# Attention over a small memory and a channel mix: nine tokens a partition, 32x64 tiles, one PSUM pool

## The chip, the core and the metric

The kernel runs on one core of a Trainium2 chip. A core has TensorE (PE, matmuls; its weight loads are listed as PEld), VectorE (DVE), ScalarE (ACT), GpSimd (POOL) and SyncE (SP). They run at the same time, each works through its own instructions in order, and they wait for each other by semaphores. 16 DMA engines move data between DRAM and the on-chip memory SBUF. TensorE writes its results to PSUM, from where DVE or ACT fetch them. The metric is the device time of one execution in microseconds.

## What is computed

Inputs are q, k, v of 8 batches x 8 heads x 576 tokens x 64, and phi of 8 x 8 x 576 x 32, all float32. Per batch and head, the attention goes over 32 memory slots:

```python
a = exp(phi - max(phi)); a = a / (sum_over_tokens(a) + 1e-09)
k_m = einsum('bhsm,bhsd->bhmd', a, k)
v_m = einsum('bhsm,bhsd->bhmd', a, v)
scores = q @ k_m.T / sqrt(64)
attn = softmax(scores)            # over the 32 slots
x = attn @ v_m                    # then heads side by side: (8, 576, 512)
```

Then a channel mix works on x, with x_prev the token before (zeros for the first):

```python
xk = mu_k * x + (1 - mu_k) * x_prev
xr = mu_r * x + (1 - mu_r) * x_prev
k = maximum(xk @ w_k, 0)          # w_k 512 x 1024
v = k * k @ w_v                   # w_v 1024 x 512
out = sigmoid(xr @ w_r) * v       # w_r 512 x 512
```

Each token needs its predecessor within its batch, and nothing else ties tokens of the channel mix together.

## The kernel before

**Two halves that are woven into each other.** `attention(b)` gives the small steps of one batch, `channel_mix(c)` sixteen groups of matmuls for one of nine chunks of 512 tokens: eight of keys (`pk`, L528), four of gates (`pr`, L542), four of values (`pv`, L561). A chunk is not a batch: chunk 1 needs batches 0 and 1. The transposed inputs of the channel mix, `xkT` and `xrT`, are a ring of four batches.

**The order is written out by hand.** Tables `STEADY` and `FIRST` give each step of a batch a position, counted in groups of the channel mix; all are sorted by it and issued. Since every engine keeps that order, a step that waits holds up all that stands behind it on its engine. After each name, letters say which PSUM pool its tiles come from: three tiles "at", two "pk" (shared with the keys), three "pv" (shared with gates and values). `busyN` steps are matmuls on zeros (L217), whose result nobody reads.

**Loads.** Of k and v, 512 tokens lie four to a partition on 128 partitions, and a tail of 64 tokens on 64 partitions as a fifth slot (L132 and L136). q lies six tokens to a partition on 96 partitions (L143), phi as k. Those of batch 0's phi go through SP's queue (L122, L125), all others through POOL's, which also turns q, k, v and the weights from float32 into bfloat16. At the start the order is k, q, v of batch 0, w_k in two parts, w_r, then phi, k, q of batch 1, w_v, v of batch 1. Tiles of q, k, v and phi exist twice, so batch b + 2 is loaded (step `load`) when batch b is done with them.

**One batch.** `exp` makes `em` = exp(phi) on ACT (L257, and L258 for the tail). `kv` (or `k` and `v` apart) multiplies it with k and v, on 128 rows x 32 columns of the array, a head's 32 slots each (L273). `z` sums `em` over tokens with a matmul against ones (L283), a reciprocal gives `rz`. `nk` scales the keys by it (L292), `tk` transposes them (L314, L317). `q0` to `q3` transpose q, two heads each (L334 on TensorE, the copy at L338); for batches 6 and 7 `qx` does it by DMA on SP (L326). `s0`, `s1` make scores of four heads, in two halves of 288 tokens, and their exp (L351, L355). `l0` to `l3` sum over the slots with a matmul and take Ln (L365, L367), `r0z` or `h0z` exponentiate its negative (L372), `w` or `y` multiply (L379): that is the softmax.

For batches 2 to 7, `nv` scales the values and masks them so that two heads' values stand side by side in 128 columns (L303). `x0` to `x3` multiply: two matmuls, each on 64 rows (two heads) x 128 columns (L392), which ACT copies out as `x` (L396). DVE then takes differences of neighbours (`dd`, L405 to L408) and mixes (`k0d` and the like, L417, L418).

For batches 0 and 1, the mix goes into the values instead: `nkx`, `nrx` multiply the values with mu and 1 - mu (L427), `mk0` to `mr3` multiply the weights of attention with both, and add the shifted one in PSUM (L449, L453), and the result is copied to `xkT` and `xrT` (L458).

**Channel mix.** ACT makes relu of the keys (L532), DVE the square (L533). The gate is exp, Ln, exp on ACT (L547 to L550). DVE multiplies gate and value (L563), and SP stores `o` (L509), the last two tiles with ACT's help.

Of the kernel before, what the change touches and what calls it, by code (L numbers as in the profile page):

```python
# [10 lines left out]
F32 = mybir.dt.float32  # L11
BF16 = mybir.dt.bfloat16
# [5 lines left out]
STEADY = [("exp", -20), ("q2", -16), ("q3+a", -15), ("kv+v", -14), ("z+v", -12), ("nk", -12), ("nv", -12),  # L18
          ("q0", -11), ("q1+a", -11), ("tk+v", -11), ("s1+aa", -8), ("s0+va", -8), ("load", -6),
          ("l0+k", -6), ("l1+k", -5), ("l3+a", -5), ("r0z", -5), ("w0", -3), ("l2+a", 1), ("r1z",  # L20
          1), ("w1", 1), ("x3+ak", 4), ("x0+av", 4), ("x2+vv", 6), ("x1+aa", 6), ("dd", 6), ("r0d",
          8), ("k2d", 11), ("k0d", 13), ("r2d", 22)]
FIRST = {
    0: [("exp", -62), ("z+k", -56), ("busy1_653415", -56), ("mub", -55), ("k+k", -53), ("mu", -48), ("nk",
        -46), ("tk+v", -44), ("q0+v", -43), ("q1+a", -40), ("q3+a", -40), ("s0+a", -39), ("q2+k",
        -38), ("l0+a", -35), ("h0z", -35), ("l1+a", -32), ("busy2_658043", -27), ("mum0", -27),
        ("s1+kv", -25), ("h1z", -25), ("v+v", -24), ("l3+v", -24), ("y0", -24), ("y1", -24),
        ("l2+v", -22), ("h2z", -22), ("busy2_100606", -20), ("h3z", -19), ("nkx", -15), ("load+a",
        -8), ("y2", -7), ("y3", -7), ("busy2_335180", -5), ("mk1+a", -5), ("mk0+kk", -5), ("mk2+aa",
        -4), ("mum1", -3), ("busy1_305423", -2), ("mk3+vv", -1), ("nrx", -1), ("mr2+aa", 2),  # L30
        ("busy1_343727", 3), ("mr0+vv", 3), ("mr1+ka", 4), ("mr3+av", 4)],
    1: [("exp", 5), ("z+a", 7), ("k+a", 9), ("q0+v", 9), ("q2+k", 9), ("nk", 9), ("q1+k", 9), ("q3+a", 9),
        ("tk+v", 9), ("s0+ak", 9), ("s1+va", 9), ("l0+v", 10), ("l1+k", 10), ("l3", 10), ("h0z",
        10), ("y0", 12), ("l2+a", 13), ("v+k", 13), ("h1z", 13), ("nrx", 13), ("nkx", 13), ("y1",
        13), ("h2z", 13), ("y2", 13), ("h3z", 13), ("y3", 13), ("mr0+va", 15), ("mk0+kv", 15),
        ("mr1+ka", 15), ("mk1+vv", 15), ("mr3+kk", 15), ("mk2+aa", 15), ("mk3+vv", 15), ("mr2+av",
        15), ("load+k", 16)],
    2: [("exp", -4), ("q0", -1), ("q1+v", -1), ("q3+a", 0), ("z+k", 0), ("kv+v", 0), ("nk", 0), ("tk+v",
        1), ("q2", 1), ("s0+kv", 2), ("s1+va", 2), ("l0+v", 3), ("l1+a", 3), ("load+k", 3), ("r0z",
        4), ("w0", 5), ("nv", 5), ("l3+a", 5), ("l2+v", 5), ("r1z", 6), ("x0+a", 8), ("w1", 9),  # L40
        ("x1+av", 10), ("x2+aa", 10), ("x3+kk", 10), ("dd", 12), ("k0d", 13), ("k2d", 13), ("r0d",
        13), ("r2d", 21)],
    3: [("exp", -4), ("z+a", -2), ("kv+v", -1), ("nk", -1), ("nv", 0), ("q0+v", 1), ("tk+a", 2), ("q1+v",
        3), ("q3", 3), ("q2", 4), ("s0+ka", 4), ("s1+ak", 5), ("l1+a", 5), ("l2+v", 5), ("l0+v", 5),
        ("l3+k", 5), ("r0z", 5), ("w0", 5), ("r1z", 5), ("w1", 6), ("x0+ka", 7), ("x1+va", 7),
        ("x2+vv", 8), ("x3+kk", 8), ("dd", 9), ("k2d", 9), ("load+k", 9), ("k0d", 11), ("r2d", 13),
        ("r0d", 15)],
    6: [("exp", -23), ("qx", -21), ("kv+v", -15), ("z+v", -12), ("nk", -12), ("nv", -12), ("tk+v", -11),
        ("load+k", -11), ("s1+va", -9), ("s0+va", -9), ("l1+k", -6), ("l0+k", -5), ("r0z", -5),
        ("l2+k", -5), ("l3+a", -4), ("w0", -3), ("r1z", 1), ("w1", 1), ("x1+av", 3), ("x0+vv", 5),  # L50
        ("x3+aa", 6), ("x2+vv", 6), ("dd", 7), ("r0d", 7), ("k0d", 12), ("k2d", 13), ("r2d", 19)],
    7: [("exp", -19), ("z+k", -12), ("kv+a", -12), ("nk", -12), ("tk+v", -11), ("nv", -11), ("qx", -8),
        ("s0+va", -8), ("s1+ak", -8), ("load+k", -8), ("l1+k", -6), ("l0+k", -6), ("r0z", -5),
        ("w0", -4), ("l2+a", -4), ("l3+a", -4), ("r1z", -4), ("w1", -4), ("x0+va", -1), ("x3+aa",
        -1), ("x2+vv", 5), ("x1+av", 5), ("dd", 7), ("r0d", 9), ("k0d", 12), ("k2d", 13), ("r2d",
        20)],
}
LOADS = {None: ("phi", "k", "v", "q"), 2: ("phi", "k", "q", "v"), 3: ("phi", "k", "q", "v"), 4: ("phi", "k", "q", "v")}
ORDER = ('phi', 'k', 'q', 'wv', 'v')

NQ = 6
JT = (0, 2, 4, 1, 3, 5)
NB = 4
TAIL = 512
# [3 lines left out]
def kernel(  # L71
# [23 lines left out]
    NT = S - TAIL  # L95
    HALF = S // 2
    QR = S // NQ
# [11 lines left out]
    NJ = NB + 1  # L109
    kvs = [const.tile([128, 2, H, NJ, D], BF16, name=f"kv{i}") for i in range(2)]  # L110
    qs = [const.tile([QR, H, NQ, D], BF16, name=f"q{i}") for i in range(2)]
    ems = [const.tile([128, NJ, H, M], BF16, name=f"em{i}") for i in range(2)]
# [6 lines left out]
    def load_phi(b, eng):  # L119
        phm = ld.tile([128, H, NB, M], F32, name="phm", tag="phm")  # L120
        pht = ld.tile([NT, H, M], F32, name="pht", tag="pht")
        eng.dma_start(  # L122
            out=phm.rearrange("p h j m -> p h (j m)"),
            in_=phi[b, :, 0:TAIL, :].rearrange("h (p j) m -> p h (j m)", j=NB))
        eng.dma_start(out=pht, in_=phi[b, :, TAIL:S, :].rearrange("h s m -> s h m"))  # L125
        loads[b] = {"phm": phm, "pht": pht}

    def load_rows(dst, src, parts=1):
        n = H // parts
        for i in range(parts):  # L130
            h = slice(i * n, (i + 1) * n)
            nc.gpsimd.dma_start(  # L132
                out=dst[:, h, 0:NB, :].rearrange("p h j d -> p h (j d)"),
                in_=src[h, 0:TAIL, :].rearrange("h (p j) d -> p h (j d)", j=NB))
            if i == 0:
                nc.gpsimd.dma_start(out=dst[:NT, :, NB, :],  # L136
                                    in_=src[:, TAIL:S, :].rearrange("h s d -> s h d"))

    def load_q(b, parts=1):
        n = H // parts  # L140
        for i in range(parts):
            h = slice(i * n, (i + 1) * n)
            nc.gpsimd.dma_start(  # L143
                out=qs[b % 2][:, h].rearrange("p h j d -> p h (j d)"),
                in_=q[b, h].rearrange("h (p j) d -> p h (j d)", j=NQ))

    def load_batch(b):
        for what in LOADS.get(b, LOADS[None]):
            if what == "phi":
                load_phi(b, nc.gpsimd)  # L150
            elif what == "q":
                load_q(b)
            else:
                load_rows(kvs[b % 2][:, "kv".index(what)], (k, v)["kv".index(what)][b])

    load_phi(0, nc.sync)
    load_rows(kvs[0][:, 0], k[0])
    load_q(0, 2)
    make_identity(nc, identity)
# [453 lines left out]
```

## Time and profile before

Three runs: 223.22, 223.40 and 223.44 us. One execution was profiled.

| | us |
|---|---|
| median of the runs | 223.4 |
| span of the profiled execution, first to last instruction | 219.9 |
| PE busy | 202.9 |
| ACT busy | 161.5 |
| DVE busy | 138.8 |
| first matmul (L283) starts | 6.45 |
| first keys of chunk 0 (L528) that run on end | 23.04 |
| first keys of chunk 1 | 52.55 |
| last product of DVE (L563) starts | 215.99 |

The time of a run has some 3.5 us more than the span, which lie around the first and the last instruction. A profile has a row of instructions for each engine: from it come the busy time of an engine, its idle time with what ended it, and the chain of waits, which goes back from the last instruction to whatever released it. Matmuls overlap, and the profile models their ends; a mean of 379 ns for a 512-column matmul does not say that one follows another at that distance. In the chain, four dense ones take 0.86 us.

The DMA queue of POOL moved 20.91 MB in 35,248 packets, its packets took 64.1% of the span of 16 engines. SP's and ACT's moved the 9.44 MB of output and batch 0's phi. Over the span DRAM was read at 38.54 MB: q, k, v and the weights are twice as large there as in SBUF.

### The profile page before, as it was taken

How to read it: one execution, taken by the hardware profiler on the slowest of the kernel's cores; microseconds unless marked ns; L12 is line 12 of the kernel's file. 1: busy time of each engine (PE TensorE's matmuls, PEld its weight loads, DVE VectorE, ACT ScalarE, POOL GpSimd, SP SyncE). 2: the span in 40 equal slices, each digit the busy share in tenths (PEclk: the TensorE clock that was granted, in tenths of full speed). 3: DMA queues.
4: the chain of work that ended last, by engine and by line, in shares of the span. 5: the costliest groups of instructions: out<-in, count | busy, mean ns of one | idle time of the engine just before them, and what ended most of it. 6: DMA issues, size and time to landing. Idle time of an engine off the chain costs nothing.

```text
span 219.9 us, 4457 instructions
## 1 busy us (share of the span) xinstructions
PE 202.9 (92%) x1698; PEld 99.5 (45%) x1698; DVE 138.8 (63%) x346; ACT 161.5 (73%) x311; POOL 47.7 (22%) x66
## 2 busy tenths in 40 slices
PE   0489997998999998999999999999999999999992
PEld 0244344446444564445444854453444444444442
DVE  3246754189465989787968677868876775425322
ACT  2256678855699849997799789988997866765770
POOL 7643351544440538211600000000000000000000
PEclk9999998799999999999999999999999999999998
DMA  6999999999999999999997700371023033033024
GB/s 139 193 191 207 238 203 203 233 223 285 210 235 196 252 243 206 229 194 289 177 180 165 174 0 3 95 174 32 13 85 97 3 95 95 0 95 98 0 64 127
DMA packets 48021, 32.67 MB, mean 149 GB/s; under 512 B 15624, under 2 KB 42512, under 8 KB 48000
## 3 DMA queue, kind: packets, MB, share of 16 engines
q0 software_dynamic: 35248, 20.91, 64.1%
q1 hardware_dynamic: 12448, 11.15, 19.0%
q10 hardware_dynamic: 304, 0.33, 0.4%
q8 instruction: 13, 0.21, 0.4%
q14 instruction: 8, 0.07, 0.1%
HBM read 38.54 MB, written 9.44 MB: 218 GB/s over the span
## 4 chain that ended last, share of the span: by engine, by line
PE 84%; DMA 5%; DVE 4%; POOL 2%; ACT 2%; issue 1%; POOLq 0%
PE pv L561 28%; PE pk L528 28%; PE pr L542 15%; DMA kv<-in_v_dram 5%; PE kvps L273 3%; PE qtps L334 2%; PE nops L392 2%; PE zps L365 2%; PE scps L351 1%; DVE qT L338 1%; PE zps L283 1%; PE mxps L449 1%; PE idle L217 1%; ACT rl L532 1%; POOL kv L132 1%
## 5 line engine op out<-in xcount | busy, mean ns | idle before, releaser
L528 PE MATMUL pk<-xkT,wk 128*128 128x512 bf16 (+1 forms) x320 | 69.0, 358 | 0.5 <-ACT rl L532 0.2
L561 PE MATMUL pv<-wv,sq 128*128 128x512 bf16 (+1 forms) x296 | 65.9, 373 | 0.0
L532 ACT ACTIVATE rl<-pk 128x512 bf16<-128x512 f32 x72 | 43.0, 601 | 26.2 <-PE pk L528 23.9
L563 DVE TENSOR_TENSOR o<-sg,pv 128x512 f32<-128x512 f32 (+1 forms) x37 | 24.1, 671 | 35.1 <-ACT sg L550 20.2
L533 DVE TENSOR_TENSOR sq<-rl 128x512 bf16<-128x512 bf16 x72 | 30.2, 423 | 24.4 <-ACT rl L532 23.8
L561 PEld LDWEIGHTS <-sq 128*128 128x128 bf16 x296 | 28.7, 98 | 32.8 <-issue 0.7
L528 PEld LDWEIGHTS <-wk 128*128 128x128 bf16 x320 | 29.4, 98 | 28.1 <-issue 2.7
L542 PE MATMUL pr<-wr,xrT 128*128 128x512 bf16 x144 | 36.4, 391 | 0.0
L547 ACT ACTIVATE sg<-pr 128x512 f32<-128x512 f32 x36 | 21.5, 609 | 7.0 <-PE pr L542 6.9
L542 PEld LDWEIGHTS <-xrT 128*128 128x128 bf16 x144 | 13.8, 100 | 16.0 <-issue 1.9
L549 ACT ACTIVATE sg<-sg 128x1024 f32<-128x1024 f32 x18 | 19.0, 1057 | 0.6
L550 ACT ACTIVATE sg<-sg 128x1024 f32<-128x1024 f32 x18 | 19.0, 1057 | 0.6
L417 DVE TENSOR_SCALAR mu_d<-diff,mu 128x576 bf16<-128x576 bf16 x48 | 16.0, 376 | 0.1
L396 ACT CAST x<-nops 128x288 bf16<-128x288 f32 x48 | 15.7, 419 | 0.2 <-PE nops L392 0.2
L379 DVE TENSOR_TENSOR atn<-e,lz 128x576 bf16<-128x576 bf16 (+1 forms) x20 | 12.4, 634 | 2.2 <-ACT lz L372 1.9
L367 ACT ACTIVATE lz<-zps 128x288 f32<-128x288 f32 x32 | 11.5, 410 | 0.9 <-PE zps L365 0.9
L338 DVE COPY qT<-qtps 128x576 bf16<-128x576 bf16 x22 | 9.3, 449 | 4.3 <-PE qtps L334 4.3
L355 ACT ACTIVATE e<-scps 128x288 bf16<-128x288 f32 x32 | 10.9, 438 | 1.1 <-PE scps L351 1.1
L372 ACT ACTIVATE lz<-lz 128x576 f32<-128x576 f32 (+1 forms) x20 | 11.4, 592 | 0.2
L257 ACT ACTIVATE em<-phm 128x1024 bf16<-128x1024 f32 x8 | 8.4, 1049 | 3.3 <-DMA phm<-in_phi_dram 3.3
L334 PE MATMUL qtps<-identity,q 96*128 96x96 bf16 x144 | 9.6, 218 | 1.0 <-DMA q<-in_q_dram 1.0
L132 POOL DMA_DIRECT2D kv<-in_v_dram x9 | 7.8, 869 | 9.8 <-issue 4.7
(67 smaller groups left out, 186.1 us busy)
## 6 DMA issues: line engine op xcount, KB each, us to landing
out_dram<-o SPq DMA_DIRECT2D x23, 192.0 KB, 2.5
kv<-in_k_dram POOLq DMA_DIRECT2D x8, 512.0 KB, 12.3
q<-in_q_dram POOLq DMA_DIRECT2D x7, 576.0 KB, 15.0
phm<-in_phi_dram POOLq DMA_DIRECT2D x7, 512.0 KB, 13.5
kv<-in_v_dram POOLq DMA_DIRECT2D x7, 512.0 KB, 14.2
out_dram<-o SPq DMA_DIRECT2D x23, 128.0 KB, 2.5
out_dram<-o SPq DMA_DIRECT2D x23, 64.0 KB, 2.3
wk<-in_moe_w_k_dram POOLq DMA_DIRECT2D x2, 512.0 KB, 12.6
```

The source lines that it names most:

```text
L334: nc.tensor.matmul(ps[:, i, j], rhs=identity[:QR, :QR], is_transpose=True, lhsT=qs[b % 2][:, 2 * pr + i, 2 * j:2 * j + 2, :].rearrange("p ...
L396: nc.scalar.copy(st["x"][:, 2 * c + jj, sl], pss[jj])
L417: nc.vector.tensor_scalar_mul(t[:, i], st["d"][:, pr + i, :], mu1[:, o:o + 1])
L528: nc.tensor.matmul(pk[:, lo:hi], lhsT=wk_sb[:, di, fi * 128:(fi + 1) * 128], rhs=xk_T[:, di, c0:c0 + hi - lo], start=(di == 0), stop=(di = ...
L532: nc.scalar.activation(rl, pk, AF.Relu)
L533: nc.vector.tensor_mul(st["sq"][:, fi, :], rl, rl)
L542: nc.tensor.matmul(pr, lhsT=xr_T[:, di, c0:c0 + 128], rhs=wr_sb[:, di, :], start=(di == 0), stop=(di == ND - 1))
L547: nc.scalar.activation(sg[:, ts % 2], pr, AF.Exp, scale=-1.0)
L549: nc.scalar.activation(sg, sg, AF.Ln, bias=1.0)
L550: nc.scalar.activation(sg, sg, AF.Exp, scale=-1.0)
L561: nc.tensor.matmul(pv[:, cols], lhsT=st["sq"][:, fi, ts * 128:(ts + 1) * 128], rhs=wv_sb[:, fi, cols], start=(fi == 0), stop=(fi == NF - 1))
L563: nc.vector.tensor_mul(o[:, cols], st[ts // 2][:, ts % 2, cols], pv[:, cols])
```

## The change

Every load of q, k, v and phi is laid out anew. A partition has nine consecutive tokens of one head; heads 0 to 3 lie on partitions 0 to 63, heads 4 to 7 on 64 to 127. There is no tail. Each load is done in two halves (phi's second in two pieces), and within heads 4 to 7 phi's are swapped in pairs, so that heads stand where the tiles later want them. Batch 0's phi goes through SP and ACT. The halves of tokens are 320 and 256 now (`HALVES`: five and four of the nine).

Loads at the start come in the order of `PRE`: batch 0's k and q half by half, its v, w_k in three pieces, w_r, phi of batch 1, half of w_v, then k, q, v of batch 1, and the other half of w_v. mu is loaded in one small tile and spread by a matmul with a selection matrix instead of four broadcasting loads.

`kv` takes nine rounds of 64 rows x 32 columns, heads of both halves in turn. q is transposed in 36 pieces of 64 rows x 64 columns instead of 24. `nv` and `nr0`/`nk0` have no mask any more: values stay 64 wide. `x` and `mk`/`mr` multiply head by head, on 32 rows x 64 columns (`head_tiles`).

All PSUM tiles come from one pool of eight, in turn. `qT`, `kmT`, `kbd`, `rz`, `e`, `atn`, `x` have three buffers instead of two, `sq` two instead of one, `o` four instead of three. The order is a list of every step and group (`PLAN`). Chunk 0's values are done in halves of columns, the odd ones early. For batches 0 and 1, most steps exist for each half of the heads. 25 `busy` matmuls instead of nine, 13 of them first of all.

```diff
-STEADY = [("exp", -20), ("q2", -16), ("q3+a", -15), ("kv+v", -14), ("z+v", -12), ("nk", -12), ("nv", -12),
...
+PLAN = [
+    "0:busy1 0:busy1 0:busy1 0:busy1 0:busy1 0:busy1 0:busy1 0:busy1 0:busy1 0:busy1 0:busy1 0:busy1 0:busy1 0:exp0",
+    "6:load 0:hk0 0:z0 0:hn0 0:ht0 0:exp1 0:hq0 0:z1 0:s0 0:hk1 0:busy1 0:l0 0:busy1 0:l1 0:busy1 0:h0z 0:hn1 0:ht1",
+    "0:h1z 0:hq1 0:y0 0:mub 0:mu 0:s1 0:hv0 0:nk0 0:busy1 0:l2 0:nr0 0:busy1 0:y1 0:l3 0:hv1 0:nk1 0:h2z 0:y2",
+    "0:busy1 0:h3z 0:y3 0:mk1 0:mk0 0:nr1 0:mk2 0:load 0:mk3 0:mr0 7:load c0:1 c0:0 c0:3 c0:2 0:mr3 0:mr1 0:mr2",
+    "c0:6 c0:7 c0:4 1:exp0 c0:8 c0:10 c0:5 c0:9 c0:11 c0:15 1:exp1 c0:13 1:z0 c0:19 1:hk0 1:hn0 1:hq1 1:hq0 0:busy1",
+    "1:ht0 0:busy1 1:z1 1:hk1 1:s0 0:busy1 0:busy1 1:l0 1:hv0 1:hn1 1:ht1 1:nr0 0:busy1 1:l1 1:h1z 1:y1 1:h0z 1:y0",
+    "1:s1 1:hv1 1:nk0 1:load 1:nr1 c0:17 1:l3 1:mr0 1:mk0 1:mk1 1:l2 c0:12 c0:14 1:h3z 1:nk1 1:h2z 1:y2 1:y3 c0:16",
+    "c0:18 1:mk3 1:mr2 1:mk2 2:exp c1:8 c1:1 c1:9 c1:0 c1:3 c1:2 c1:5 2:z 1:mr3 1:mr1 c1:4 0:busy1 2:q1 2:kv 2:nk",
...
-ORDER = ('phi', 'k', 'q', 'wv', 'v')
+PRE = "k0:0 q0:0 k1:0 q1:0 id: v0:0 v1:0 wk:0-2 wk:2-4 wk:4-8 wr:0-4 phi:1 wv:2-4 k0:1 q1:1 q0:1 k1:1 v0:1 v1:1 wv:0-2"
...
-NQ = 6
-JT = (0, 2, 4, 1, 3, 5)
+NJ = 9
+JT = (0, 2, 4, 6, 8, 1, 3, 5, 7)
...
+    def rows(src, hg):
+        return src[hg * HH:(hg + 1) * HH].rearrange("h (p j) d -> p h (j d)", j=NJ)
+
+    def load_phi(b, engs):
+        ph = ld.tile([128, HH, NJ, M], F32, name="ph", tag="ph")
+        engs[0].dma_start(out=ph[ROWS[0]].rearrange("p h j m -> p h (j m)"), in_=rows(phi[b], 0))
+        src = rows(phi[b], 1).rearrange("p (a i) x -> p i a x", i=2)
+        dst = ph[ROWS[1]].rearrange("p (a i) j m -> p i a (j m)", i=2)
+        for i in range(2):
+            engs[1].dma_start(out=dst[:, i], in_=src[:, 1 - i])
+        loads[b] = ph
+
+    def load_rows(dst, src, halves=(0, 1)):
+        for hg in halves:
+            nc.gpsimd.dma_start(out=dst[ROWS[hg]].rearrange("p h j d -> p h (j d)"), in_=rows(src, hg))
...
         def ps_tile(shape, dtype, name):
-            tags = st["tags"]
-            tag = {"a": "at", "k": "pk", "v": "pv"}[tags[st["n"] % len(tags)]]
-            st["n"] += 1
-            return psum.tile(shape, dtype, name=name, tag=tag, bufs={"at": 3, "pk": 2, "pv": 3}[tag])
+            return psum.tile(shape, dtype, name=name, tag="ps", bufs=8)
...
                 for j in range(NJ):
-                    for h in range(H):
-                        c, g = divmod(h, 4)
-                        nc.tensor.matmul(kvps[g * M:(g + 1) * M, c], lhsT=em[:, j, h, :],
-                                         rhs=kv5[:, parts, h, j, :],
-                                         start=j == 0 and c == 0, stop=j == NB,
-                                         skip_group_check=True)
+                    for g in range(HH):
+                        for c in cs:
+                            nc.tensor.matmul(kvps[c][g * M:(g + 1) * M], lhsT=em[ROWS[c], j, g, :],
+                                             rhs=kv5[ROWS[c], parts, g ^ c, j, :],
+                                             start=j == 0, stop=j == NJ - 1,
+                                             skip_group_check=True)
...
+        def head_tiles(c, pss, src, lo, hi, cols=slice(0, None), **flags):
+            for g in range(HH):
+                r, i = slice(g * M, (g + 1) * M), (g + c) % 2
+                nc.tensor.matmul(pss[g // 2][i * D:(i + 1) * D, cols], lhsT=src[r, c], rhs=st["at"][r, c, lo:hi],
+                                 skip_group_check=True, **flags)
...
+        def tr_q(i):
+            def go():
+                pss = [ps_tile([128, NJ, QR], BF16, "qtps") for _ in range(2)]
+                for n in range(NJ):
+                    n0 = 2 * (NJ * i + n)
+                    for hg in range(2):
+                        r = ROWS[hg]
+                        nc.tensor.matmul(pss[hg][:, n], rhs=identity[r, r], is_transpose=True,
+                                         lhsT=qs[b % 2][r, n0:n0 + 2, :].rearrange("p n d -> p (n d)"),
+                                         start=True, stop=True, skip_group_check=True)
+                for hg in range(2):
+                    (nc.scalar.copy if b < 2 and hg else nc.vector.tensor_copy)(
+                        q_tile()[:, hg, NJ * i:NJ * (i + 1)], pss[hg])
+            return go
...
-                pss = [ps_tile([128, HALF], F32, "scps") for _ in range(2)]
-                for g in range(4):
+                pss = [half_tile(hf, "scps") for hf in range(2)]
+                for g in (0, 2, 1, 3):
                     m = slice(g * M, (g + 1) * M)
                     for hf in range(2):
-                        r = slice(hf * D, (hf + 1) * D)
+                        n = [NJ * (g ^ c) + j for j in JT[5 * hf:5 + 4 * hf]]
+                        r = ROWS[n[0] % 2]
...
         def values(c, hf):
...
-                pss = []
-                for jj in range(2):
-                    r = slice(jj * 64, (jj + 1) * 64)
-                    ps = ps_tile([128, HALF], F32, "nops")
-                    nc.tensor.matmul(ps, lhsT=st["vbd"][r, c].rearrange("p h d -> p (h d)"),
-                                     rhs=st["at"][r, c, sl], start=True, stop=True)
-                    pss.append(ps)
+                pss = [half_tile(hf, "nops") for _ in range(2)]
+                head_tiles(c, pss, st["vb"], sl.start, sl.stop, start=True, stop=True)
...
         def mixed(w, c, hf):
...
+                vm = st["vm", w]
+                head_tiles(c, pss, vm[:, 0], lo, hi, start=True, stop=False)
+                for n, (c0, c1, p0) in enumerate(before[hf]):
+                    head_tiles(c, pss, vm[:, 1], p0, p0 + c1 - c0, slice(c0 - lo, c1 - lo),
+                               start=False, stop=n == len(before[hf]) - 1)
```

Steps of `PLAN` are read as batch:step, or c and the chunk:group; groups 0 to 7 are keys, 8 to 11 gates, 12 and up values. `hk`, `hv`, `hn`, `ht`, `hq` are the steps of before for one half of the heads; `6:load` and `7:load` do nothing, as there is no batch 8 or 9.

## The prediction

> **What bounds the kernel now.** I read the page's slices first, then the chain of waits in order of time, then busy time by stretches.
>
> ```profile
> PE 202.9 (92%) x1698; PEld 99.5 (45%) x1698; DVE 138.8 (63%) x346; ACT 161.5 (73%) x311; POOL 47.7 (22%) x66
> ...
> PE   0489997998999998999999999999999999999992
> ...
> PEclk9999998799999999999999999999999999999998
> DMA  6999999999999999999997700371023033033024
> ```
>
> TensorE is the bound, except in the first four slices of 5.5 us. The loads keep the 16 DMA engines full until slice 21 (some 118 us), which is no wait by itself: TensorE reads 9 long before that. The chain says what the first slices wait for:
>
> ```profile
> 6.28 10.64 DMA kv<-in_v_dram
> 16.97 0.67 PE kvps L273 x27
> ...
> 19.94 0.35 PE mxps L449 x2
> 20.49 0.40 ACT xkT L458
> 21.74 0.43 DVE mu_m L238
> ...
> 23.04 2.10 PE pk L528 x9
> ```
>
> Batch 0's values land at 16.97; the keys of chunk 0 (pk) really run from 23.04. Now the stretches; columns are length, then busy us of PE, PEld, DVE, ACT, POOL, granted clock, DMA share, GB/s:
>
> ```profile
> 17.00:23.04 6.04, 5.75 (x67) 2.49 (x67) 4.78 (x14) 3.71 (x11) 2.47 (x4) 1.00 1.24 214
> 23.04:52.50 29.46, 27.66 (x285) 13.60 (x285) 16.72 (x47) 21.56 (x44) 11.11 (x15) 0.94 1.38 224
> 52.50:80.00 27.50, 27.28 (x303) 13.80 (x301) 19.55 (x50) 20.89 (x41) 10.94 (x14) 1.00 1.37 231
> 80.00:91.00 11.00, 10.01 (x113) 5.07 (x112) 8.64 (x24) 9.39 (x25) 6.29 (x8) 1.00 1.38 234
> 91.00:216.00 125.00, 124.92 (x837) 60.45 (x834) 83.00 (x187) 99.85 (x181) 5.51 (x7) 1.00 0.50 99
> ```
>
> A busy PE is not a PE at its peak, so I count what had to be done. In the chain four dense 512-column matmuls take 0.86 us, 0.216 each. The channel mix is 720 of them (320 pk of which 64 are halves, 288 pv, 144 pr): 155.5 us, fixed by the arithmetic. The attention pieces, from the chain, are about 3.5 us a batch and some 26 in all. 155.5 + 26 of 219.9 leaves 38 us that are neither: 17 before 20 us, 4 in the tail (216 to 219.9), and 17 between. From 91 us on, with 0.08 idle in 125, only the changes between kinds of matmul are lost. What can be won lies before 91. In 23.04 to 52.50 chunk 0 (80 x 0.216 = 17.3), batch 1's attention (3.1) and 60 mixing matmuls (3.9) make 24.3 of 29.5: 5.2 are lost, a third of it to the clock (0.94 of 29.5 us: 1.8). In 80 to 91 the chain leaves TensorE for ACT and DVE (83.45 to 89.2), and some 2.6 are lost.
>
> **The change part by part.** Sums are against the execution's own 219.9; the median of 223.4 lies 3.5 above it, which I keep.
>
> *Loads in halves of 64 rows, nine tokens a partition.* A batch's k was 1,024 runs of 512 B and 512 of 128 B as they land, q 768 of 768 B; now all are 512 runs of 1,152 B. I take 210 GB/s from the stretches (214 and 224; the first 10 us had 162, the next 197). A half of k, q or v is 295 KB: 1.4 us. Before, phi and k (1.17 MB) were there at 8.91, so at 210 the stream stands as if begun at 3.3. After: phi, k and q (1.77 MB) by 11.7; v (2.36 MB) by 14.5 against 16.97; all of batch 0, batch 1 and the weights (7.3 MB) by 38. POOL's issues rise from 7 to 9 a batch at some 0.7 us, and nothing waits on POOL but loads.
>
> *The start.* q's second half at 11.7, 18 transposes and two copies (0.46 DVE, 0.64 ACT) give s1 at about 13.2, where the trace has 16.17. From s1 to pk the trace took 6.9 (two exp of 0.36, two Ln, two reciprocals, two products, mix, copies); POOL's and SP's issues are not in it. I charge 5.3: with all keys and queries there, half 0's softmax no longer waits in the same queue, and `mk` needs v only at 14.5. So pk at 18.5 instead of 23.0: **-4.5**. Bounds: 0 if ACT's queue, in which half 0's softmax still precedes half 1's, keeps the 6.9 and more, and -6. The nearest row is the 6.9, hence nearer to -4.5 than to -6. wk's first quarter lands at 15.8, before pk, and holds nothing up. The four memsets and 16 of DVE's mask steps go (2 us before 6 us, DVE waits anyway: nothing). Eight of 16 `vm` products at 342 ns go, 2.7 us of DVE in two batches; beside TensorE, nothing.
>
> *Fillers.* 13 instead of one in front. A filler takes 427 ns cold, 13 take 5.5 us and end at 6.7, just when k's first half can be there: at most +0.5 if they hold it up. Before, four fillers at 18.23 still took 1.71 us (427 each, twice the 216), so the start ran at half speed; 0.5 less there is inside the bounds above. In 33 to 42 the granted clock fell to 0.81, among waits for L292 and L317; fillers stand there now, which is part of the next item.
>
> *Chunk 0 and batch 1.* 24.3 us of work from 18.5 would end at 42.8. But batch 1's last key half lands about 34, scores, softmax, mix cost some 6 to 7 from there, and the order puts only five value halves and some mixing (5.8 us) beside it: I put chunk 1 at 46.5, before 52.5. That is **-1.5** beyond the start; bounds 0 and -5.
>
> *80 to 91.* One pool of eight PSUM tiles for pools of 3, 2 and 3, and three buffers for e, atn, x, q: scores no longer wait in the two-tile queue. I take **-1** of 2.6; bounds +1 (ACT runs at 9.9 of 10 us in places and gets no less work: `em` 8 x 1,049 + 8 x 404 becomes 10 of about 1,150) and -2.6.
>
> *Transposes of q.* 24 of 96 columns become 36 of 64. By
>
> ```profile
> L334 PE MATMUL qtps<-identity,q 96*128 96x96 bf16 x144 | 9.6, 218 | 1.0 <-DMA q<-in_q_dram 1.0
> ...
> L392 PE MATMUL nops<-atn,vbd 64*128 64x288 bf16 x48 | 5.2, 288 | 0.5 <-DVE atn L379 0.3 <-ACT rl L532 0.2
> ...
> L273 PE MATMUL kvps<-kv,em 128*32 128x128 bf16 x240 | 4.5, 220 | 0.0
> ```
>
> and the chain's 12 in 0.51 (42 ns each, 96 columns), 64 columns cost 29: 1.04 a batch one by one, as before, or 0.52 if the two row halves run side by side. Four batches lie on TensorE's path: 0 to -2, taken **-1**.
>
> *Keys and values of phi (kvps).* 40 matmuls of 128 rows become 72 of 64. The chain has 40 in 0.67: 4 column tiles side by side, 57 ns a round. 72 on 8 tiles are 9 rounds: 0.52 + the same end, **0**. Here a rule speaks against the change: "TensorEngine Tiling (Array Packing)", Instruction Overhead, gives each matmul about 60 cycles whatever its columns, 25 ns[...]. 32 more in 8 batches, 12 in 6, 48 + 80 in values and mix would be 456 x 25 ns = +11.4 us. The row says 17 ns for one of 128 columns, and batch 1's 40 of 64 columns took 0.42, 10 ns each. Different tiles overlap; I go by the row, and 72 x 10 = 0.72 is the dear end (+0.05 a batch).
>
> *32x64 tiles for values and mix.* Per step two matmuls on 64x128 tiles become four on 32x64. The chain has four L392 in 0.35, two rounds of 122 and a change of kind. Four tiles side by side make one round of 133 (320 columns) or 107: the same columns, **0**. Second rule: the same page, PSUM Pressure, has different row tiles barred from one PSUM bank at the same time. `head_tiles` writes heads 0 and 1, from two row tiles, into the two halves of one tile, so one bank. The trace never does that (L392's and L351's row tiles have a bank each). Below nothing is excluded: the columns are the same. By the rule each step has a second round: values 6 x 0.48 = 2.9; mix 2 x 1.9 = 3.8; scores, whose row tiles swap banks midway, 16 x 0.13 = 2.1: +8.8. I take 0, since the halves are different partitions, and keep 8.8.
>
> *The rest.* SP's two DMA transposes (3.1 us each) become four of half size; stores queue behind them, covered by four `o` buffers instead of three. Without the cover: up to 1.5 us once. The tail is the same pv halves and stores: 0.
>
> Sum: -4.5 - 1.5 - 1 - 1 = **-8.0**: span 211.9, time **215.4**.
>
> **Rivals.**
> - *Shared bank (slower).* Row tiles of one bank take turns. +8.8 against -8.0 gives 224.2; in the order 0, 1, 2, 3 it can be three rounds, up to +15.6: 231. It decides from 8 us, that is if every step doubles. For it: the rule, and scores now issued 0, 2, 1, 3. Against: separate partitions. 16%.
> - *The start is given back.* ACT's queue or the landings hold pk at 22 and batch 1 at 50: -4.5 and -1.5 become -1.5 in all, sum about -3.5: 219.9 (219 to 223). For it: ACT's work is unchanged, and DMA moved 224 GB/s before too. 14%.
> - *No gap at all to chunk 1.* 42.8 instead of 46.5, transposes in pairs: -12.5, 210.9 (209 to 212.5). Against it: 34 + 6 for batch 1. 12%.
> - *No effect:* 2%.
> - *Forecast:* 212.5 to 219, 56%.
>
> **Numbers.** Under 0.2% cannot be told from no change here. Faster 56 + 14 + 12 = 82%, same 2%, slower 16%. The range, 210 to 222, drops the slower case and the ends of the two others: 80% inside.
>
> **What would show it.** Right: first pk of chunk 0 at 18 to 19, chunk 1's keys at 45 to 48; four nops matmuls starting within 20 ns, a pair of steps in about 0.35 us; 72 kvps in 0.5 to 0.7; PE idle under 1 us in the stretch that answers to 80 to 91. Wrong: nops starts 107 to 133 ns apart within a step (shared bank), v's landing after 16 us, or waits for L360 and L372 (exp, Ln) before chunk 1.

## The result, and the profile after

The changed kernel takes 216.28 us in the median of four runs (214.22 to 217.12), the kernel before 223.31 in the runs beside them (221.99 to 223.44): a ratio of 0.9681 (0.9626 to 0.9737), some 7.0 us faster. Forecast were 215.4 us, within 210 to 222. Runs more than 1.5% above the fastest of their kernel stay out of the ratios; of all the kernels here only one had such runs, two of its four (the transposes one half after the other).

In every execution here the time is 1.7 to 1.9 us above the span, not 3.5: 217.12 goes with a span of 215.4, 221.69 with 219.9. The two profiled executions are therefore an unequal pair: the changed kernel's is its slowest of four, and the one of before (219.9) was none of the three runs shown with it, but one of some 221.7 us, at the low end of what before took in later comparisons (221.4 to 224.5). The two profiles differ by 4.5 us, the medians by 7.0.

From the page of the changed kernel, busy time and the slices of 5.4 us:

```profile
PE 207.0 (96%) x2280; PEld 107.1 (50%) x2280; DVE 133.5 (62%) x338; ACT 161.9 (75%) x307; POOL 48.0 (22%) x81
...
PE   7699999899999999999899999999999999999992
...
PEclk9855999679999999999999999999999999999998
...
q0 software_dynamic: 18480, 20.91, 54.0%
```

The empty slices at the start are full now, but some of that is fillers and a slow clock: PEclk is 5 in the third and fourth slice and 6 in the eighth. POOL's queue moves the same 20.91 MB in 18,480 packets instead of 35,248, with 54.0% of the DMA engines' time instead of 64.1%. The same by stretches (columns as in the prediction): start to the first keys of chunk 0, those to the first matmul of chunk 1, from there nearly to the end, and 80 to 91 by itself.

```profile
0.00:21.50 21.50, 18.40 (x296) 10.58 (x296) 8.62 (x37) 10.79 (x21) 12.07 (x23) 0.70 1.10 193
21.50:51.80 30.30, 29.61 (x432) 17.63 (x429) 14.56 (x43) 21.45 (x41) 12.55 (x20) 0.87 1.22 222
51.80:211.50 159.70, 159.04 (x1563) 78.93 (x1555) 109.88 (x262) 129.62 (x246) 23.39 (x38) 1.00 0.64 132
80.00:91.00 11.00, 11.00 (x142) 5.18 (x141) 10.41 (x29) 10.91 (x23) 3.03 (x5) 1.00 1.14 242
```

PE is without a gap in 80 to 91, where 10.01 of 11 were busy before. Set against the three terms of the forecast, with the lengths from the timelines of both profiles (before: 23.04, then 29.51 to chunk 1 at 52.55, then 163.13 to the last matmul at 215.68):

| stretch | forecast | before | after | change |
|---|---|---|---|---|
| start to first pk | -4.5 | 23.04 | 21.51 | -1.5 |
| first pk to chunk 1 | -1.5 | 29.51 | 30.31 | +0.8 |
| chunk 1 to last matmul | -2 | 163.13 | 159.37 | -3.8 |
| last matmul to the end | 0 | 4.2 | 4.2 | 0 |

The medians are near the forecast, then, but in this pair nearly all was won behind chunk 1, and what was promised ahead of it is missing. The steady part is seen in the chain of waits of the changed kernel, at batches 2 to 4, and of the kernel before:

```profile
67.63 0.63 PE qtps L322 x36
...
70.30 0.44 PE nops L285 x8
70.74 0.73 PE kvps L239 x72
...
83.42 0.27 PE nops L285 x8
...
85.62 0.25 PE nops L285 x8
```

```profile
74.42 0.67 PE kvps L273 x40
...
77.18 0.51 PE qtps L334 x12
...
105.77 0.35 PE nops L392 x4
```

36 transposes of q take 0.63 where 24 took 1.02, and 72 kvps 0.73 where 40 took 0.67. A pair of values' steps (nops) is eight small matmuls in 0.24 to 0.44, where it was four large ones in 0.35 to 0.42.

The missing start is seen in the timeline of PE (start, us, what, count):

```profile
11.49 0.61 PE L197 MATMUL idle<-zeros 128*128 128x512 bf16 x1
...
12.16 0.63 PE L197 MATMUL idle<-zeros 128*128 128x512 bf16 x1
...
12.80 0.63 PE L197 MATMUL idle<-zeros 128*128 128x512 bf16 x1
13.23 0.31 PE L298 MATMUL ktps<-identity,kbd 128*128 128x128 bf16 x1
13.47 1.14 PE L338 MATMUL qtps<-identity,q 64*128 64x64 bf16 x18
14.54 1.22 PE L203 MATMUL mub<-mu_r,sel 4*128 4x128 f32 x4
...
15.70 0.47 PE L356 MATMUL scps<-qT,kmT 64*32 64x320 bf16 x8
```

The second half's scores (s1) come at 15.70, not 13.2, and no wait is shown in front of them. PE works through its queue: three fillers (L197), a transpose of keys, 18 of q at 59 ns each, and the four float32 matmuls that spread mu.

### The profile page after: what moved, and what is told of

The parts are those of the page before. It is cut to its first block, busy times and chain, and to the rows that moved or that the text cites. A ratio compares the mean times of both kernels' runs of the same rounds, so it can differ in the third digit from the quotient of the medians.

```text
span 215.4 us, 5652 instructions
## 1 busy us (share of the span) xinstructions
PE 207.0 (96%) x2280; PEld 107.1 (50%) x2280; DVE 133.5 (62%) x338; ACT 161.9 (75%) x307; POOL 48.0 (22%) x81
## 3 DMA queue, kind: packets, MB, share of 16 engines
q0 software_dynamic: 18480, 20.91, 54.0%
## 4 chain that ended last, share of the span: by engine, by line
PE 79%; DMA 15%; POOL 1%; ACT 1%; issue 1%; DVE 0%; POOLq 0%
PE pv L554 28%; PE pk L519 26%; PE pr L533 13%; DMA ph<-in_phi_dram 7%; DMA wv<-in_moe_w_v_dram 5%; DMA q<-in_q_dram 3%; PE kvps L239 3%; PE zps L370 2%; PE nops L285 2%; PE scps L356 1%; PE qtps L322 1%; PE mxps L285 1%; POOL kv L114 1%; PE idle L197 1%; PE zps L248 1%
## 5 line engine op out<-in xcount | busy, mean ns | idle before, releaser
L554 PEld LDWEIGHTS <-sq 128*128 128x128 bf16 x328 | 31.8, 99 | 30.4 <-issue 1.4
L396 ACT CAST x<-nops 128x256 bf16<-128x256 f32 (+1 forms) x48 | 15.7, 429 | 2.7 <-PE nops L285 2.7
L372 ACT ACTIVATE lz<-zps 128x320 f32<-128x320 f32 (+1 forms) x32 | 12.0, 417 | 5.3 <-PE zps L370 5.3
L114 POOL DMA_DIRECT2D kv<-in_k_dram x16 | 10.1, 634 | 22.8 <-PE nops L285 9.4
L360 ACT ACTIVATE e<-scps 128x320 bf16<-128x320 f32 (+1 forms) x32 | 10.7, 412 | 5.2 <-PE scps L356 5.2
L114 POOL DMA_DIRECT2D q<-in_q_dram x16 | 9.9, 621 | 19.6 <-PE qtps L322 9.0
L227 ACT ACTIVATE em<-ph 128x1152 bf16<-128x1152 f32 (+1 forms) x10 | 11.6, 1158 | 2.7 <-DMA ph<-in_phi_dram 2.7
L384 DVE TENSOR_TENSOR atn<-e,lz 128x576 bf16<-128x576 bf16 (+2 forms) x20 | 12.3, 632 | 1.9 <-ACT lz L377 1.9
L197 PE MATMUL idle<-zeros 128*128 128x512 bf16 x25 | 11.5, 563 | 1.2 <-DVE zeros L129 1.2
L408 DVE TENSOR_TENSOR diff<-x 128x1024 bf16<-128x1024 bf16 (+1 forms) x18 | 9.0, 553 | 4.5 <-ACT x L396 4.5
## 6 DMA issues: line engine op xcount, KB each, us to landing
q<-in_q_dram POOLq DMA_DIRECT2D x16, 288.0 KB, 10.2
wv<-in_moe_w_v_dram POOLq DMA_DIRECT2D x2, 512.0 KB, 13.4
```

Source lines behind the costliest of these rows:

```text
L114: nc.gpsimd.dma_start(out=dst[ROWS[hg]].rearrange("p h j d -> p h (j d)"), in_=rows(src, hg))
L396: nc.scalar.copy(st["x"][:, 2 * c + jj, sl], pss[jj])
L554: nc.tensor.matmul(pv[:, cols], lhsT=st["sq"][:, fi, ts * 128:(ts + 1) * 128], rhs=wv_sb[:, fi, cols], start=(fi == 0), stop=(fi == NF - 1))
```

## The experiments

All kernels below compute the whole reference. Each comparison has its own runs of the kernel before, and ratios are to those; the comparisons were taken on different chips. "pk" is the first keys of chunk 0, "chunk 1" its first matmul, "rest" from there to the last matmul; in the changed kernel they are 21.51, 51.82 and 159.4. In some kernels below the first key is followed by a wait of 0.2 us, and the next comes 0.8 to 1.0 us after it; pk is then the first.

**Without fillers.** All 25 `busy1` steps are taken out of `PLAN`.

```diff
-    "0:busy1 0:busy1 0:busy1 0:busy1 0:busy1 0:busy1 0:busy1 0:busy1 0:busy1 0:busy1 0:busy1 0:busy1 0:busy1 0:exp0",
-    "6:load 0:hk0 0:z0 0:hn0 0:ht0 0:exp1 0:hq0 0:z1 0:s0 0:hk1 0:busy1 0:l0 0:busy1 0:l1 0:busy1 0:h0z 0:hn1 0:ht1",
+    "0:exp0",
+    "6:load 0:hk0 0:z0 0:hn0 0:ht0 0:exp1 0:hq0 0:z1 0:s0 0:hk1 0:l0 0:l1 0:h0z 0:hn1 0:ht1",
...
```

> The changed kernel without all 25 filler matmuls. If fillers keep the clock up, the half clock lasts longer than the 13.7 + 6.8 us of the profile and the time rises by 1 to 3 us. If they only stand in front of work (the clock is at half from 8.7 to 22.3 us in spite of them), the waits behind them go and the time falls by 0.5 to 1.5 us.

Measured: 213.68 us (212.90 to 213.96), ratio 0.9597 (0.9555 to 0.9640). Its timeline of PE at the place shown above:

```profile
12.21 1.14 PE L338 MATMUL qtps<-identity,q 64*128 64x64 bf16 x18
...
14.44 0.47 PE L356 MATMUL scps<-qT,kmT 64*32 64x320 bf16 x8
...
18.99 1.25 PE L519 MATMUL pk<-xkT,wk 128*128 128x512 bf16 x5
```

Up to the second half's kvps the two kernels run alike: these start at 10.55 here and at 10.64 with fillers, so the 13 in front cost nothing. Between there and pk the plan has six more, three before s1 and three behind it. At 427 ns each, that is 1.28 before s1 (15.70 against 14.44: 1.26) and 2.56 in all (21.51 against 18.99: 2.52). The fillers stand in PE's own queue on the path, and the path has to wait for each. In this pair they brought no clock in return: the 18 transposes take 1.14 us in both. The time fell as the second theory had it, but by 2.6 us by the medians where it put at most 1.5.

The 2.5 us are not the same in every execution. Batch 1's early kernel, below, has the start of the changed kernel to the letter, fillers too, and its clock was back at full at 13.4 us:

```profile
13.29 0.75 PE L338 MATMUL qtps<-identity,q 64*128 64x64 bf16 x18
...
18.67 0.82 PE L519 MATMUL pk<-xkT,wk 128*128 128x512 bf16 x2
```

The five kernels with this order of the start had half clock there for 3.4 to 13.7 us, and pk follows it: 18.67 and 19.45 with 3.4 (the latter is the kernel with five PSUM tiles), 20.54 and 20.76 with 10.2 (transposes one half after the other, values on 64x128 tiles), 21.51 with 13.7 (the changed kernel). So fillers cost their length while the clock is at half, and can be worth nothing net where it comes back early; without them pk was at 18.92 and 18.99 in the two kernels that change nothing else there.

**More fillers.** The twelve behind the first line become `busy3`.

```diff
-    ... 0:hk1 0:busy1 0:l0 0:busy1 0:l1 0:busy1 0:h0z 0:hn1 0:ht1",
+    ... 0:hk1 0:busy3 0:l0 0:busy3 0:l1 0:busy3 0:h0z 0:hn1 0:ht1",
```

> The changed kernel with each of the 12 fillers after the first 13 made three matmuls. If the half clock from 8.7 to 22.3 and 39.4 to 46.2 us comes from too little TensorE work in those stretches, the granted clock over the span rises from about 0.95 to 0.98 and the time falls by 1 to 3 us, as far as the extra 24 matmuls (5 us at full clock) stand in idle time. If they stand in the way: +2 to +5 us.

Measured: 215.36 us (215.19 to 215.51), ratio 0.9681 (0.9635 to 0.9727). The page's clock line and the two first stretches:

```profile
PEclk9969999999999999999999999999999999999998
```

```profile
0.00:21.00 21.00, 17.33 (x308) 9.45 (x308) 8.07 (x36) 10.48 (x21) 11.98 (x23) 0.92 1.10 188
21.00:50.20 29.20, 28.74 (x443) 17.31 (x439) 14.87 (x44) 21.61 (x42) 12.25 (x21) 1.00 1.23 219
```

Enough fillers do keep the clock up (0.92 and 1.00 in place of 0.70 and 0.87), and 18 transposes take 0.69 instead of 1.14. Yet pk comes at 21.05: what the clock gains is spent on the fillers themselves. Beside the 18.99 without fillers, few cost 2.5 us at the start in this pair, many 2.1.

**Transposes one half after the other.** The two row halves of q no longer alternate.

```diff
-                for n in range(NJ):
-                    n0 = 2 * (NJ * i + n)
-                    for hg in range(2):
-                        r = ROWS[hg]
+                for hg in range(2):
+                    r = ROWS[hg]
+                    for n in range(NJ):
+                        n0 = 2 * (NJ * i + n)
```

> The changed kernel, but q is transposed half by half of the heads (18 pieces from rows 0 to 63, then 18 from rows 64 to 127) instead of alternating between them. If pieces from different rows overlap (36 in 0.63 to 0.74 us in the trace after, against 36 x 29 = 1.05 one by one), four batches lose 0.3 to 0.4 us each: +1.2 to +1.7 us against the changed kernel, 217.5 to 218, and 36 pieces again take 1.05. If the alternation brings nothing to the end of the program (another wait hides it): within 0.4 us of the changed kernel.

Measured: 215.51 us in the median of all four runs (213.0 to 219.8), ratio 0.9598 (0.9533 to 0.9663) by the two lower ones, and pk at 20.54 and chunk 1 at 50.81 although nothing before chunk 1 had been meant to change: the time decides nothing against the changed kernel. In the chain 18 take 0.53 and 36 take 0.86. It was repeated without fillers, where the start is steadier.

> The kernel without fillers (213.7 us, and steadier from run to run than the changed kernel), with q transposed half by half as in the run qserial. If pairs of pieces from different rows are worth what the trace shows (18 pieces in 0.53 instead of 0.37 us), batches 2 to 5 cost +1.0 to +1.6 us: about 215, and the stretch from chunk 1's first gate to the last matmul grows from 158.4 to 159.5 to 160 us. If the alternation is hidden: within 0.4 us of 213.7.

Measured: 215.79 us (215.13 to 216.35), ratio 0.9685 (0.9650 to 0.9720), against 0.9597 without the swap: 2.0 us by the ratios, intervals apart. The pk comes at 18.92 as without the swap; the rest is 159.5 instead of 158.4, and 158.5 in the three other kernels of the same comparison, whose transposes alternate. The chain of this kernel, then of the one without fillers whose transposes alternate:

```profile
57.96 0.53 PE qtps L322 x18
...
66.12 0.86 PE qtps L322 x36
```

```profile
56.30 0.37 PE qtps L322 x18
...
64.17 0.63 PE qtps L322 x36
```

The alternation saves 0.16 for every 18 and 0.23 to 0.32 for a batch, 1.0 for the four batches whose q TensorE transposes behind chunk 1. The rest, 1.1 longer, agrees with the chains. What the ratios show beyond it lies before chunk 1 (50.21 instead of 48.54), where this edit changes nothing: there the clock came back to full later, 14 keys from 19.75 on taking 4.06 us where 16 from 18.99 on took 3.63. So I count 1.1.

**Values on 64x128 tiles again.** `vb` gets its mask back, and `values` two matmuls a step; the mix of batches 0 and 1 stays on 32x64.

```diff
-                head_tiles(c, pss, st["vb"], sl.start, sl.stop, start=True, stop=True)
+                for jj in range(2):
+                    r = slice(jj * 64, (jj + 1) * 64)
+                    nc.tensor.matmul(pss[jj], lhsT=st["vb"][r, c].rearrange("p i d -> p (i d)"),
+                                     rhs=st["at"][r, c, sl], start=True, stop=True, skip_group_check=True)
```

> The changed kernel, but batches 2 to 7 multiply the values as before the change: masked values, two heads on 64 rows x 128 columns, two matmuls a step instead of four on 32 x 64. The columns that stream through are the same. Theory of the prediction (equal columns): nothing on TensorE, within 0.4 us. Rival (32x64 tiles are faster since the drain between kinds is shorter, 8 in 0.26 us): +0.1 us a pair of steps, 12 pairs, +1.2 us. Rival (32x64 tiles pay for a shared bank): faster by up to 2.9 us.

Measured: 216.99 us (215.95 to 218.97), ratio 0.9762 (0.9698 to 0.9827), which overlaps the changed kernel's; the rest is 159.57 beside 159.4. Its chain has, at the places shown for the changed kernel,

```profile
70.10 0.42 PE nops L403 x4
...
83.22 0.38 PE nops L403 x4
...
85.53 0.32 PE nops L403 x4
```

From the first start of a pair of steps to the next other instruction, the twelve pairs take 0.32 to 0.38 with large tiles, 4.2 in all, and with small ones 0.24 to 0.30 at nine places and 0.37 to 0.44 at three, 3.6 in all. So the small tiles save some 0.6 us on PE, half of what the first rival expected. The rests hide it, since PE stops once for 0.62 us at 105 in the changed kernel's profile and not in this one. The starts show why: four large matmuls go in two rounds, the second 108 to 146 ns after the first, while all eight small ones start within 24 ns at eight of the twelve places. The two steps of a pair lie on different tiles, and run in one round. A second round for a shared bank is not seen.

**Batch 1, or batch 0, earlier in the plan.** If the order held up batch 1, its steps should gain from standing in front of chunk 0's gates and values. A second kernel moves the sums of batch 0's first half (`l0`, `l1`) behind the preparation of the second, a third does both.

```diff
-    "c0:6 c0:7 c0:4 1:exp0 c0:8 c0:10 c0:5 c0:9 c0:11 c0:15 1:exp1 c0:13 1:z0 c0:19 1:hk0 1:hn0 1:hq1 1:hq0 0:busy1",
+    "c0:6 1:exp0 1:exp1 c0:7 1:z0 1:hk0 1:hn0 1:hq1 c0:4 1:ht0 1:hq0 1:z1 c0:8 1:s0 1:hk1 c0:10 1:l0 1:hn1",
...
-    "6:load 0:hk0 0:z0 0:hn0 0:ht0 0:exp1 0:hq0 0:z1 0:s0 0:hk1 0:busy1 0:l0 0:busy1 0:l1 0:busy1 0:h0z 0:hn1 0:ht1",
+    "6:load 0:hk0 0:z0 0:hn0 0:ht0 0:exp1 0:mub 0:mu 0:hq0 0:z1 0:s0 0:hk1 0:hn1 0:ht1 0:hq1 0:busy1 0:l0 0:s1 0:l1",
```

> The changed kernel with batch 1's attention steps moved up among the keys and gates of chunk 0 (both halves of exp(phi) right after the first keys, softmax before the second pair of gates); same work, fillers there gone. Theory A (order): by the bytes that POOL's queue had moved, batch 1's data are on the chip by about 31 us, and chunk 1 waits for ACT's queue; then chunk 1's first gate starts at 46 to 48 instead of 51.8, and the time falls by 3 to 5 us, to 211 to 213. Theory B (the landings set it, as the prediction had it: batch 1's last key half at 34, w_v at 38): steps wait for loads in front of chunk 0's own work, the time is the same or up to 3 us longer.

> The changed kernel with batch 0's second half of heads moved up (its keys, transposes and scores stand before the first half's sums, and the matmul that spreads mu before the first transposes of q); most fillers there gone. Theory A (order): s1 runs at 12.5 to 13 us instead of 15.7 and the first keys of chunk 0 at 18.5 to 19.5 instead of 21.5; the time falls by 1.5 to 3 us, unless batch 1's late start takes it back (then 0 to -1). Theory B (half clock and the chain of exp, Ln, exp set the start): keys at 21 or later, time within 0.5 us.

> Both reorderings at once. Theory A: they add, 5 to 8 us less than the changed kernel, 208 to 211 us, chunk 1's first gate at 43 to 46. Theory B: no more than 1 us less, or longer.

Measured: batch 1 early 219.32 us, ratio 0.9836 (0.9766 to 0.9906), chunk 1 at 54.78. Batch 0's order 215.74, ratio 0.9701 (0.9614 to 0.9788), pk at 19.95 and chunk 1 at 50.21, not told apart from the changed kernel. Both 217.57, ratio 0.9769 (0.9678 to 0.9860), chunk 1 at 51.63. In the timeline of the first, the brackets hold PE's idle time and what ended it:

```profile
26.10 0.37 PE L258 MATMUL zps<-ones,em 64*128 64x1 bf16 x9 [1.25 <-ACT em L227]
29.66 0.67 PE L239 MATMUL kvps<-kv,em 64*32 64x64 bf16 x36 [3.18 <-DMA kv<-in_k_dram]
31.09 1.14 PE L338 MATMUL qtps<-identity,q 64*128 64x64 bf16 x18 [0.77 <-DMA q<-in_q_dram]
```

Put earlier, batch 1's steps make PE stand still for 5.2 us, 4.0 of them for k and q and the rest for ACT's `em`, and half clock follows from 27.1 to 37.3 us. That this earlier order would gain is refuted. It does not show that the landings set chunk 1: its first half of k lands at 29.66 and a half of q at 31.09, by that distance (an estimate) its last half of k at 34, and chunk 1 comes 21 us after that, with no further wait for a load.

The two moves were tried once more without fillers, batch 0's order alone and with batch 1's second `exp` right behind its first on ACT.

> The order of the run batch0_order with no filler at all. If the order of the second half of heads and the fillers cost separately, the first keys of chunk 0 start at 17 to 18 us (18.99 without fillers alone) and the time is 212 to 213. If what is won there waits for batch 1's loads, chunk 1's first gate stays at 48 to 48.6 and the time at 213.5 to 214.

> As the run batch0_nofill, and batch 1's second exp(phi) stands on ACT right behind its first, ahead of the gates of chunk 0. If ACT's queue (gates' Ln and exp, then this exp, then the copies of q) sets batch 1's scores, chunk 1's first gate comes 0.5 to 1.2 us earlier: 211.5 to 212.5. If batch 1's q and k set it: the same as batch0_nofill; if phi's second half lands late enough to hold up the gates behind it: up to 1 us longer.

Measured: 216.46 us, ratio 0.9707 (0.9669 to 0.9746), and 216.35, ratio 0.9717 (0.9681 to 0.9753): both slower by the ratios than the kernel without fillers, where 212 to 213 was hoped for. The pk of the first comes at 21.4, where the same order with fillers had 19.95 and the old order without them 18.99; mu's matmuls, 1.19 us, now stand in front of the first transposes of q. What of it costs the 2.4 us was not separated. The place of this `exp` on ACT changes nothing (chunk 1 at 51.9 and 51.78), so it is not what holds up batch 1.

**Short runs.** Each half of k, q and v is loaded in two pieces, five and four tokens (without fillers, transposes alternate).

```diff
-            nc.gpsimd.dma_start(out=dst[ROWS[hg]].rearrange("p h j d -> p h (j d)"), in_=rows(src, hg))
+            s4 = src[hg * HH:(hg + 1) * HH].rearrange("h (p j) d -> p h j d", j=NJ)
+            for js in (slice(0, 5), slice(5, 9)):
+                nc.gpsimd.dma_start(out=dst[ROWS[hg]][:, :, js, :], in_=s4[:, :, js, :])
```

> The kernel without fillers, with every load of q, k and v cut in two along the tokens, so that runs of 640 and 512 B land instead of 1,152 (POOL issues twice as many of them). If the length of the runs is what the loads gained, a half takes some 20% longer (a packet of 512 took 60 ns, one of 1,152 took 106; 640 by the line between them 69): batch 0's v is 2 us later, batch 1's data 4 us, and the time rises by 2 to 5 us. If the DMA engines are bound by bytes: within 0.5 us.

Measured: 214.66 us (213.54 to 216.05), ratio 0.9630 (0.9588 to 0.9672), which overlaps that with long runs. POOL's queue has 31,536 packets and 63.3% of the engines' time, instead of 18,480 and 54.9%. In the profile pk comes at 20.21, where the swapped transposes of the same comparison have 18.92; but this execution was the slowest of six, 1.4 above their median. So the length of runs, together with twice the issues on POOL, is worth 1.3 us or less at the start, and in time it was not told apart from nothing; the 2 to 5 us of the first theory did not come.

**Five PSUM tiles instead of eight.**

```diff
-            return psum.tile(shape, dtype, name=name, tag="ps", bufs=8)
+            return psum.tile(shape, dtype, name=name, tag="ps", bufs=5)
```

> The changed kernel with five PSUM tiles in the one pool instead of eight. If the depth of the pool removed the wait in 80 to 91 us (2.6 us before) and others like it, the time rises by 2 to 5 us. If the order of the steps did it, within 1 us.

Measured: 238.01 us (236.93 to 239.18), ratio 1.0698 (1.0601 to 1.0795). The start is no slower (pk at 19.45, chunk 1 at 52.51), but the rest is 178.4. One row of its stretches:

```profile
52.50:231.00 178.50, 164.35 (x1539) 81.42 (x1555) 111.06 (x260) 132.18 (x245) 22.77 (x37) 1.00 0.58 117
```

PE loses 14 us to waiting, and the time rises by far more than the 2 to 5 us expected. This order needs more than five tiles. It does not say what pools of 3, 2 and 3 cost the order of before.

## Why the prediction was right in its sum and wrong in its parts

The likeliest case gave 215.4; 216.28 was measured, 0.9 more. The sum of -8.0 stands beside -7.0 by the medians. Of the signs that it named, v on the chip before 16 us came true (its first matmul runs at 14.63 without a wait in the kernel without fillers), four nops within 20 ns (the first four of every pair start within 11), a pair of steps in about 0.35 or less, and PE without idle time in 80 to 91; the two on pk and chunk 1 did not. With the kernel without fillers as a second measure, its terms are:

| term of the prediction | forecast | with fillers | without |
|---|---|---|---|
| start | -4.5 | -1.5 | -4.1 |
| chunk 0 and batch 1 | -1.5 | +0.8 | 0.0 |
| all behind chunk 1 | -2 | -3.8 | -4.7 |
| sum on the span | -8.0 | -4.5 | -8.8 |

**Start: the mechanism held, a term was mis-sized.** "13 fillers ... at most +0.5" counted those in front, and they cost nothing. The six that stand further back, between `hk1` and `mk1`, were seen only as a possible gain of the clock ("0.5 less there is inside the bounds"). They cost 2.5 in the profiled pair, at half clock. Without them pk comes at 18.99 beside the forecast 18.5, and 4.1 of the 4.5 are there. (Before has seven fillers of its own behind its first kvps, so part of the 4.1 may be theirs; it was not separated from what the new loads and the work on halves bring.) Its inner steps were off in opposite senses: s1 at 14.44 instead of 13.2, with the 18 transposes at half speed and mu's matmuls in front of it, and then 4.55 to pk instead of 5.3.

**Chunk 0 and batch 1: wrong.** 46.5 for chunk 1 came from landings at 34 plus 12.5 us. The landings fit, as the early batch 1 shows. But the path from there takes longer: in the changed kernel batch 1's keys start at 36.1, the clock is at half from 39.4 to 46.2, and five fillers stand among its steps. Without fillers chunk 1 starts at 48.54, pk to chunk 1 is 29.55, as long as before (29.51), with 1.7 us of waits (for `kbd`, `em` and `e`) and 6.8 us at half clock. Before had 3.4 us at half clock in this stretch, so an estimate of what the clock took is 1.7 us, as much as the term promised. The kernel with more fillers had full clock here and took 29.16 from pk to chunk 1 with 15 fillers of 0.216 in it, which leaves 26, less than the forecast's 28 (46.5 less 18.5). So the clock, which 34 plus 12.5 left out, can explain the miss; no run separates it from the waits.

**80 to 91: right.** Put at -1 of 2.6. Of these, the trace shows 1.0 as idle time of PE (10.01 of 11 busy), and that went; the rest of the 2.6 was an estimate. Whether the pool, the third buffers or the new order did it was not separated.

**Transposes of q: right.** Put at -1. The chain has 0.63 to 0.74 instead of 1.02 for four batches, 1.1 to 1.6, and undoing only the alternation lengthens the rest by 1.1. What the rest won beyond these two terms stands in pieces that were put at 0: counted from each start to the next, idle time left out, the values fell from 4.3 to 3.6 us and the scores from 2.8 to 2.0. The -4.7 without fillers differ from the -3.8 by the stop of 0.62 and by one filler.

**kvps: right at about 0. The 32x64 tiles: somewhat better than 0.** 72 kvps in 0.73 is the dear end, 0.06 a batch. The Trainium skill, "TensorEngine Tiling (Array Packing)", Instruction Overhead, gives a matmul an overhead of about 60 cycles; that is 25 ns at the 0.42 ns a column of these traces (0.216 us for 512). Added up matmul by matmul it made +11.4, which did not come: 72 kvps on eight tiles take 10 ns each. Nor did the +8.8 of the same page's PSUM Pressure, by which different row tiles cannot access one bank at the same time. A pair of values' steps has eight matmuls in four banks, two row tiles in each; with large tiles and a bank for each row tile the last round and the change of kind behind it take some 0.20 us, and the eight small ones take 0.24 to 0.30 in all at nine of twelve places, where a second round would add 0.11 to 0.14 (256 or 320 columns). Row tiles that write different partitions of one bank run side by side here, so the rival of the shared bank is out. The "0" for these tiles counted one round a step; as the two steps of a pair share a round, it was 0.6 us too dear.

**Start given back.** This rival's sum (-3.5) is near to what the profile pair shows (-4.5), and its pk at 22 nearly came true (21.51); but not by its mechanism. Neither ACT's queue nor the landings held pk, but fillers at half clock; and the gain behind chunk 1, which it had at -2, made up for it.

**No gap at all.** This rival did not come. Its sum was also off: with its own terms (-4.5, -5.2, -1 and -2) it is -12.7 and not -12.5.

**The 3.5 us around the span** were no such thing: 1.8 lie there, and 1.7 was the distance of the profiled execution from the median of other runs. The terms were worked out on an execution at the low end and set against a median 1.7 higher; from that execution's own time, -8.0 would have been 213.7. Part of the nearness is luck: the terms ahead of chunk 1 missed by 3.0 and 2.3 us, the one behind it was exceeded by 1.8, and the changed kernel's clock moves its runs by 2.9.

**The version that beats both** is the changed kernel without its fillers: 213.68 us, ratio 0.9597 (0.9555 to 0.9640), 2.6 us below the changed kernel by the medians. The two intervals overlap a little (0.9626 to 0.9640), but the fastest run of the changed kernel (214.22) lies above the slowest of this one (213.96), and in the profiled pair 2.5 us are found at the six fillers.

## What to carry to other kernels

Count every instruction that stands in the path's own queue, fillers too: one that warms nothing costs its full length, twice as long at half clock, and one in front of a load that is not there yet costs nothing. When a total comes out as forecast, compare its terms stretch by stretch; in this pair one was over by 3 us, one by 2, and a third under by 2. Before a profile's span is set against a median, ask which run it belongs to.

## What the hardware showed unexpectedly

- Fillers of 5.0 us in front warmed the clock briefly: the first 36 kvps take 0.44 us behind them and 0.67 without. Then the records give half clock from 8.7 to 22.3 us in the changed kernel, although PE is 9 tenths busy with small matmuls in most of that. With the same order of the start it lasted 3.4 us in two other kernels and 10.2 in two more. Why it fell there, and what sets how long it lasts, was not found.
- The granted clock reads 1.00 until the first record. The kernel without fillers shows 1.00 for its first 19 us, while its transposes run at the same 1.14 us for 18 as the changed kernel's at a recorded 0.50. In the start the durations tell the clock, not the column.
- Transposes from two row halves in turn overlap, 36 in 0.63 us; one half after the other, 0.86.
- Eight matmuls on eight 32x64 tiles start within 24 ns and take one round, though each two row tiles share a PSUM bank.
- The changed kernel's own runs differ by 2.9 us (214.22 to 217.12), in step with the mean clock of each (0.983 to 0.948). Without fillers four runs lie within 1.1 us.
